# A fused linear-attention and MLP kernel: the transposes of x for units 5 and 6 on SyncE's DMA queue in place of TensorE

## The chip, the cores and the metric

The kernel runs on 1 core of a Trainium2 chip. The metric is the device time of one execution in microseconds (us). The kernel before took 170.78 us, the median of 3 runs (170.48 to 170.87).

## The reference

Two stages are fused. The first is a gated linear attention over 4 batches, 8 heads, 768 steps and a head size of 48; the second is a two-layer MLP with squared ReLU on its 3072 x 384 output.

```python
for t in range(S):                                   # S = 768
    state = alpha[:, :, t, :, None] * state + einsum('bhd,bhe->bhde', k[:, :, t], v[:, :, t])
    y[:, :, t] = einsum('bhd,bhde->bhe', q[:, :, t], state)
x = y.transpose(0, 2, 1, 3).reshape(B * S, H * D)    # 3072 x 384
h = x @ w_in                                         # 384 x 2048
r = maximum(h, 0); g = r * r
out = g @ w_out                                      # 2048 x 384
```

## The kernel before

The 3072 tokens are cut into 12 units of 256 tokens, numbered 0 to 11; four batches take turns, so unit g is chunk g // 4 of batch g % 4. For each unit g the kernel does, in this order (the names are those of the tables in `ORDERS`, and the lines those of the profile):

- `lda`, `ldk`, `ldq`, `ldv`: load alpha, k, q and v, 384 KB each, into one of four `raw` buffers, number g % 4 (L540).
- `pr`, `ln`, `m1`, `ei`, `ea`, `es`, `bk`, ...: the decays; `eqm0`, `eqm1` (L732) and `ekm` (L737) multiply them into q and k and write `qks`, buffer g % 3.
- `tr0`, `tr1` (L748): from unit 3 on, two DMA transposes on SyncE's queue turn `qks` into `kqt`, buffer g % 3.
- `p0` (L926): the scores on TensorE, which read `kqt`; `mk0`, `mk1` (L937) mask them.
- `y` (L818, L829, L797): the attention's output and the next state on TensorE; `xe` (L957) copies it as bf16 into `xbf`, buffer g % 2.
- `xt`: x, 128 x 768 in bf16, is turned for the MLP. Up to unit 6 TensorE does it with six 128 x 128 transposing matmuls (L972) into PSUM, and `xv` (L984) copies the result into the `xt` buffer g % 4. From unit 7 on a single DMA transpose on SyncE's queue (L978) writes that buffer directly, and there is no `xv`. The tuple `DMA_X` holds the units that take this second way.
- `s1_g_0` to `s1_g_7` (L1030): the first layer, six matmuls each, reading `xt`; `re` (L1038, L1040) is its ReLU and `sq` (L1052, L1048, L1051) the square.
- `s2_g_...` (L1168, L1096): the second layer, for units 3 to 10 by Strassen's scheme, whose sums are `ga`, `gb`, `gc` and whose results are gathered by `ca` to `cg`; `out` stores 384 KB.

The order of the work on every engine is written out by hand in five tables in `ORDERS`, one for each engine; each engine runs its row from left to right and waits on semaphores where it needs another's result. `fill` names small matmuls on zeros in the first 16 us (L1231). Several units are under way at a time: while TensorE computes the first layer of unit 5, the attention of unit 6 and the loads of units 7 and 8 are running. SyncE's table is one queue: whatever waits at its head holds everything behind it.

The switch between the two ways for x is in `output`:

```python
if g in DMA_X:
    to = XT[s][:].rearrange("p k j t -> p (k j t)").rearrange("p (a t) -> p a t", t=128)
    add("sp", lambda e: e.dma_start_transpose(to, src), 1300, p0 + 6700, reads=[("xbf", x2)],
        writes=[("xt", s)], name=f"xt{g}", dma=f"x{s}", lag=1400)
    return
add("pe", xtr, pe_ns(6, 128), p0 + 6700, reads=[("xbf", x2), ("ident",)], writes=[("ps", "X", 0)], name=f"xt{g}")
```

Of the kernel before, what the change touches and what calls it, by code (L numbers as in the profile page):

```python
# [34 lines left out]
        cd6 eqm0_10 eqm1_10 ga7_0 ce6 sa10 ga7_1 cg6 re8_4 cf6 re8_5 ca7 cb7 lb11 ekm11 eqm0_11 eqm1_11 mk0_10 cd7
        mk1_10 ce7 cf7 re9_1 ga8_1 cg7 re9_2 sa11 ca8 re9_4 mk0_11 re9_7 cb8 mk1_11 re10_0 cd8 ga9_1 ce8 gb9_1 re10_2
        ga9_0 cg8 cf8 re10_7 cb9 cc9 ga10_0 cd9 gc9_0 ce9 ga10_1 cf9 cg9 cb10 re11_4 gc10_0 cd10 ce10 cg10 re11_6
        sq11_7 cf10 oe11_0 oe11_11
    """,
    "pe": """  # L40
        fill512_0 fill512_1 fill512_2 fill512_3 fill512_4 fill512_5 fill256_6 m10_0 m11_0 fill512_7 tr00_0 tr10_0
        fill512_8 fill256_9 fill256_10 tr01_0 p0_0 tr11_0 kv0 fill256_11 p1_0 fill512_12 m11 y0 fill512_13 fill512_14
# [1 line left out]
        kv1 s1_0_3 y1 s1_0_4 s1_0_5 xt1 s1_0_7 s1_0_6 m1i2 s1_1_2 s1_1_1 m1s2 s1_1_0 s1_1_4 s1_1_5 s1_1_3 s1_1_7 tr0_2
        s1_1_6 s2_0_0_0 tr1_2 s2_0_0_1 s2_0_1_0 p0_2 s2_0_1_1 s2_0_0_2 s2_0_0_3 kv2 s2_0_1_2 m1i3 s2_0_1_3 s2_1_0_0
        s2_1_0_1 m1s3 y2 m1i4 s2_1_0_2 xt2 s2_1_0_3 s1_2_0 s1_2_1 s2_1_1_0 s2_1_1_1 s1_2_2 s1_2_3 p0_3 s2_1_1_2 s1_2_5
        s1_2_4 s2_1_1_3 y3 s1_2_6 s1_2_7 xt3 m1i5 s2_2_0_0 s1_3_1 s2_2_0_1 s1_3_0 p0_4 s2_2_0_2 s1_3_3 s2_2_0_3 s1_3_2
        s1_3_5 y4 s2_2_1_0 s1_3_4 m1i6 s1_3_7 xt4 s2_2_1_1 s2_2_1_2 s1_3_6 s2_2_1_3 s1_4_1 p0_5 s1_4_0 s2_3_m10 s1_4_3
        s2_3_m11 s1_4_2 y5 s2_3_m20 s1_4_4 m1i7 s2_3_m60 s2_3_m61 s2_3_m21 xt5 s1_4_6 s2_3_m70 s1_4_5 s2_3_m50
        s2_3_m71 s2_3_m51 s1_4_7 p0_6 s2_3_m40 s1_5_0 s1_5_1 s2_3_m30 s1_5_2 s2_3_m41 s1_5_3 s2_3_m31 y6 s2_4_m10  # L50
        s2_4_m60 s2_4_m11 s1_5_5 m1i8 xt6 s2_4_m61 s1_5_4 s2_4_m20 s2_4_m21 s1_5_7 s1_5_6 p0_7 s2_4_m70 s1_6_1 s1_6_0
        s2_4_m50 s2_4_m71 s2_4_m51 s1_6_2 y7 s2_4_m30 s2_4_m40 s2_4_m41 s1_6_3 m1i9 s1_6_4 s2_4_m31 s2_5_m60 s1_6_5
        s2_5_m10 s2_5_m11 s1_6_6 s1_6_7 s2_5_m61 p0_8 s2_5_m20 s2_5_m21 s1_7_1 s1_7_0 s2_5_m70 s2_5_m71 s1_7_3 s1_7_2
        s2_5_m50 s2_5_m51 s2_5_m40 y8 s2_5_m41 s2_5_m30 s1_7_4 s2_6_m60 m1i10 s2_5_m31 s1_7_5 s2_6_m61 s2_6_m10
        s2_6_m11 s1_7_6 s1_7_7 p0_9 s2_6_m20 s2_6_m70 s1_8_0 s2_6_m21 s2_6_m71 s1_8_1 s1_8_2 s2_6_m50 y9 s2_6_m51
        s2_6_m40 s1_8_3 s2_6_m30 s2_6_m31 s1_8_4 s2_6_m41 s2_7_m10 m1i11 s1_8_5 s2_7_m60 s2_7_m11 s2_7_m61 s1_8_6
        s2_7_m20 s1_8_7 s2_7_m70 s2_7_m21 p0_10 s2_7_m50 s2_7_m51 s2_7_m71 s1_9_0 s1_9_1 s2_7_m40 s2_7_m41 s1_9_2 y10
        s2_7_m30 s2_7_m31 s1_9_3 s2_8_m10 s2_8_m60 s2_8_m11 s1_9_5 s1_9_4 p0_11 s2_8_m20 s1_9_7 s2_8_m61 s2_8_m21
# [1205 lines left out]
```

## Time and profile before

| | |
|---|---|
| median of 3 runs | 170.78 us |
| the profiled execution | 169.46 us, of which 167.7 us from the first to the last instruction |
| granted TensorE clock | 1.000 |
| busy | TensorE 96%, VectorE 79%, ScalarE 72%, GpSimd 58% of the span |
| DMA moved | 32.80 MB, mean 196 GB/s |

In the profile's rows PE is TensorE, PEld its weight loads, DVE VectorE, ACT ScalarE, POOL GpSimd, and SPq the issues of DMAs on SyncE. A row of the timeline has the start, the duration, the engine, the source line, the operation and what it writes and reads; a trailing x2 joins two alike. An SPq row's duration is that of the issue alone; when the data have landed is told in the DMA view, as microseconds from the issue. Times are counted from the start of the span.

### The profile page before, as it was taken

The numbers are of one execution on the slowest core, as the hardware profiler recorded it, in microseconds if no ns is written. First come the engines' busy times: TensorE is split into PE (matmuls) and PEld (weight loads), VectorE is DVE, ScalarE is ACT, GpSimd is POOL, SyncE is SP. The second block draws the span as 40 slices with busy tenths as digits, with TensorE's granted clock in tenths as the row PEclk, the third lists the DMA queues.
The fourth block names the chain that finished last, engine by engine and source line by source line (L and its number), as shares of the span: only waits on it lengthen the run. The fifth ranks groups of instructions, "written<-read, shape, count | busy, mean of one in ns | idle before, by whom it ended". The sixth has DMA issues, their size and how long they took to land.

```text
span 167.7 us, 5626 instructions
## 1 busy us (share of the span) xinstructions
PE 160.9 (96%) x2431; PEld 139.6 (83%) x2431; DVE 131.9 (79%) x234; ACT 121.3 (72%) x214; POOL 96.8 (58%) x93
## 2 busy tenths in 40 slices
PE   7699999997999999999999999999999999999994
...
DMA  5999999999999999999999989989988500522022
GB/s 135 327 319 209 275 303 216 200 338 267 161 230 166 229 295 124 294 160 263 282 163 327 241 136 336 141 193 334 133 203 139 148 10 4 152 87 94 0 98 94
DMA packets 68232, 32.80 MB, mean 196 GB/s; under 512 B 64144, under 2 KB 65168, under 8 KB 68208
## 3 DMA queue, kind: packets, MB, share of 16 engines
...
q14 instruction: 5, 0.04, 0.1%
HBM read 25.17 MB, written 4.72 MB: 178 GB/s over the span
## 4 chain that ended last, share of the span: by engine, by line
PE 75%; DMA 15%; POOL 4%; DVE 3%; issue 1%; ACT 1%
PE psWH L1030 32%; PE psO L1096 13%; PE psWH L1096 10%; PE psO L1168 7%; DMA win<-in_moe_w_in_dram 7%; DMA wout<-in_moe_w_out_dram 5%; DMA raw<-in_alpha_dram 3%; PE psX L829 2%; PE psX L926 2%; PE psZ L797 2%; POOL raw L540 2%; PE psX L818 2%; PE psX L998 2%; PE psZ L926 1%; PE psX L972 1%; POOL win L508 1%
## 5 line engine op out<-in xcount | busy, mean ns | idle before, releaser
L1030 PE MATMUL psWH<-xt,win 128*128 128x256 bf16 x552 | 71.7, 273 | 0.2 <-DMA win<-in_moe_w_in_dram 0.2
L1030 PEld LDWEIGHTS psWH<-xt,win 128*128 128x128 bf16 x552 | 60.1, 129 | 2.1 <-DVE xt L984 0.4
L1038 ACT ACTIVATE rr<-psWH 128x512 bf16<-128x512 f32 x70 | 40.9, 595 | 18.3 <-PE psWH L1030 17.2
L1052 ACT ACTIVATE gt<-rr 128x1024 bf16<-128x1024 bf16 (+1 forms) x38 | 35.1, 940 | 2.8 <-PE psWH L1096 1.6
L1051 POOL TENSOR_TENSOR gt<-rr 128x512 bf16<-128x512 bf16 (+1 forms) x13 | 18.6, 1432 | 14.8 <-ACT rr L1038 9.7
L1082 POOL TENSOR_TENSOR gt<-sg,gt 128x512 bf16<-128x512 bf16 x10 | 12.0, 1202 | 12.6 <-DVE sg L1080 12.6
L1040 DVE TENSOR_SCALAR rr<-psWH 128x512 bf16<-128x512 f32 x22 | 15.0, 685 | 5.1 <-PE psWH L1030 5.0
L1168 PE MATMUL psO<-wout,gt 128*128 128x384 bf16 x96 | 18.4, 326 | 0.0
L937 DVE TENSOR_TENSOR pm<-psZ,caus 128x1024 bf16<-128x1024 f32 x12 | 14.6, 1218 | 1.9 <-PE psZ L926 1.9
L937 DVE TENSOR_TENSOR pm<-psX,caus 128x1024 bf16<-128x1024 f32 x12 | 14.6, 1215 | 0.6 <-PE psZ L926 0.5
L1096 PE MATMUL psWH<-sw,gt 128*128 128x192 bf16 x128 | 14.8, 246 | 0.0
L1096 PE MATMUL psO<-wout,gt 128*128 128x192 bf16 x128 | 14.7, 246 | 0.0
L1083 POOL TENSOR_TENSOR sh<-gt 128x512 bf16<-128x512 bf16 x11 | 14.2, 1298 | 0.7 <-DVE gt L1082 0.5
L1168 PEld LDWEIGHTS psO<-wout,gt 128*128 128x128 bf16 x96 | 8.8, 98 | 4.6
L686 POOL TENSOR_TENSOR ek<-ek,raw 128x384 f32<-128x384 f32 x7 | 7.1, 1008 | 9.6 <-ACT ek L679 9.6
L1127 DVE TENSOR_TENSOR osb<-psWH,osb 128x192 f32<-128x192 f32 x24 | 8.4, 350 | 5.0 <-PE psWH L1096 4.9
L737 DVE TENSOR_TENSOR qks<-raw,ek 128x768 bf16<-128x768 f32 x11 | 11.7, 1063 | 0.4 <-ACT ek L644 0.4
L1080 DVE TENSOR_TENSOR sg<-gt 128x1024 bf16<-128x1024 bf16 x14 | 10.6, 754 | 0.9 <-PE psO L1096 0.9
L1096 PEld LDWEIGHTS psWH<-sw,gt 128*128 128x128 bf16 x128 | 10.9, 98 | 0.3
L1096 PEld LDWEIGHTS psO<-wout,gt 128*128 128x128 bf16 x128 | 10.6, 98 | 0.5
L957 ACT ACTIVATE xbf<-psX 128x768 bf16<-128x768 f32 x11 | 8.9, 806 | 2.9 <-PE psX L818 1.7
L732 DVE TENSOR_TENSOR qks<-raw,eq 128x384 bf16<-128x384 f32 x18 | 10.4, 604 | 0.7 <-DMA raw<-in_q_dram 0.7
...
## 6 DMA issues: line engine op xcount, KB each, us to landing
out_dram<-osb SPq DMA_DIRECT2D x11, 384.0 KB, 4.8
raw<-in_alpha_dram SPq DMA_DIRECT2D x10, 384.0 KB, 5.1
raw<-in_q_dram SPq DMA_DIRECT2D x10, 384.0 KB, 5.5
raw<-in_v_dram SPq DMA_DIRECT2D x10, 384.0 KB, 4.8
raw<-in_k_dram SPq DMA_DIRECT2D x9, 384.0 KB, 5.2
...
raw<-in_k_dram POOLq DMA_DIRECT2D x3, 384.0 KB, 6.4
raw<-in_alpha_dram POOLq DMA_DIRECT2D x2, 384.0 KB, 6.0
```

The costliest lines, as they stand in the source:

```text
L737: add("dve", lambda e, a=a, E=E: e.tensor_tensor(QKS[qs][:, a, :, :, 0:D], RAW[r][:, 1 + a].rearrange("p h j d -> p j h d"), E[la][:].rear ...
L937: add("dve", lambda e, hf=hf, psT=psT: e.tensor_tensor(PM[pm][:, hf].rearrange("p r n j t -> p (r n) (j t)"), psT[:, :, :].rearrange("p r ...
L1030: ins = pe.matmul(psF[:, i * T:(i + 1) * T], WIN[:, kk, hidden(fj)], mov, start=(kk == 0), stop=(kk == KT - 1))
L1038: add("act", lambda e, psF=psF, rr=rr: e.activation(rr, psF, AF.Relu), act_ns(512), pu + 600, reads=[keyF], writes=[("rr", rb, half)], nam ...
L1040: alts={"dve": (lambda e, psF=psF, rr=rr: e.tensor_scalar(rr, psF, 0.0, None, ALU.max), dve_ns(512))})
L1051: alts={"pool": (lambda e, dst=dst, sq=sq: e.tensor_tensor(dst, sq, sq, ALU.mult), 200 + k * 840), "act": (lambda e, dst=dst, sq=sq: e.act ...
L1052: "act": (lambda e, dst=dst, sq=sq: e.activation(dst, sq, AF.Square), act_ns(k * 512))})
L1080: ga = lambda e, us=us: e.tensor_tensor(SG[:, us], view(us, 128, [[0, 2], [1, 128]]), view(us, 0, [[384, 2], [1, 128]]), ALU.subtract)
L1082: gb = lambda e, us=us: e.tensor_tensor(G4[:, us, 0, 1], SG[:, us, 1], G4[:, us, 0, 0], ALU.subtract)
L1083: gc = lambda e, us=us: e.tensor_tensor(SH[:, us], G4[:, us, 1, 0], G4[:, us, 0, 1], ALU.add)
L1096: ins = pe.matmul(psS, left(u), right(u), start=(first and u == 0), stop=(u == nu - 1), skip_group_check=True)
L1168: ins = pe.matmul(psS, GT[gt][:, fj, j, :], WOUT[:, fj, :], start=(fj == 0), stop=(fj == FT - 1))
```

## The change

`DMA_X` gets the units 5 and 6, so their two groups of six transposing matmuls leave TensorE, their two copies `xv5` and `xv6` leave VectorE, and two DMA transposes come onto SyncE's queue. The tables are changed with it, in one stretch that begins around the end of unit 3's first layer and ends at unit 6's (on SyncE between `out0_1` and `xt8`); behind it they are as before. Four `fill` matmuls are added in the first 16 us and some change their size. In the same stretch other operations move by a few places in their tables, and two change engine: `ca3` goes from ScalarE to VectorE and `gb5_1` from VectorE to GpSimd.

```diff
-    DMA_X = (7, 8, 9, 10, 11)
+    DMA_X = (5, 6, 7, 8, 9, 10, 11)
...
     "sp": """
-        ldk6 ldq6 tr1_5 tr0_5 ldv6 lda7 ldk7 lda8 tr0_6 tr1_6 ldv7 ldq7 ldq8 out1_1 ldk8 tr0_7 tr1_7 ldv8 lda9 ldk9
+        ldk7 ldk6 lda7 ldq6 tr1_5 tr0_5 ldv6 lda8 ldv7 ldq7 tr0_6 tr1_6 ldq8 xt5 ldk8 ldk9 lda9 out1_1 tr0_7 tr1_7
+        ldv8 xt6 lda10 ldq9 ldv9 tr0_8 tr1_8 out2_1 xt7 out3_1 lda11 tr1_9 tr0_9 ldk10 xt8 ldv10 ldq10 ldk11 ldq11
```

SyncE's queue behind the store of unit 0 is the first place. raw2 is the buffer of unit 6, raw3 of unit 7, raw0 of unit 8; kqt2 and kqt0 belong to units 5 and 6, xt1 to unit 5. Before, from `ldk6` to `ldq8`:

```order
L540 DMA raw2<-in_k_dram 128x8x96
L540 DMA raw2<-in_q_dram 128x8x96
L748 DMA_TRANSPOSE kqt2<-qks2 128x16x64 x2
L540 DMA raw2<-in_v_dram 128x8x96
L540 DMA raw3<-in_alpha_dram 128x8x96
L540 DMA raw3<-in_k_dram 128x8x96
L540 DMA raw0<-in_alpha_dram 128x8x96
L748 DMA_TRANSPOSE kqt0<-qks0 128x16x64 x2
L540 DMA raw3<-in_v_dram 128x8x96
L540 DMA raw3<-in_q_dram 128x8x96
L540 DMA raw0<-in_q_dram 128x8x96
```

The same place now, from `ldk7` to `xt5`:

```order
L540 DMA raw3<-in_k_dram 128x8x96
L540 DMA raw2<-in_k_dram 128x8x96
L540 DMA raw3<-in_alpha_dram 128x8x96
L540 DMA raw2<-in_q_dram 128x8x96
L748 DMA_TRANSPOSE kqt2<-qks2 128x16x64 x2
L540 DMA raw2<-in_v_dram 128x8x96
L540 DMA raw0<-in_alpha_dram 128x8x96
L540 DMA raw3<-in_v_dram 128x8x96
L540 DMA raw3<-in_q_dram 128x8x96
L748 DMA_TRANSPOSE kqt0<-qks0 128x16x64 x2
L540 DMA raw0<-in_q_dram 128x8x96
L978 DMA_TRANSPOSE xt1<-xbf1 128x6x128
```

Two loads of unit 7 (k and alpha) have moved ahead of the transposes of unit 5, two more (v and q) ahead of those of unit 6, and `xt5` stands behind exactly the eleven rows that were there before, in another order.

The second place is SyncE's queue behind that. raw1 is the buffer of unit 9, kqt1 of unit 7, xt2 of unit 6. Before, from `out1_1` to `ldk9`:

```order
L1184 DMA out_0_dram<-osb1 128x768
L540 DMA raw0<-in_k_dram 128x8x96
L748 DMA_TRANSPOSE kqt1<-qks1 128x16x64 x2
L540 DMA raw0<-in_v_dram 128x8x96
L540 DMA raw1<-in_alpha_dram 128x8x96
L540 DMA raw1<-in_k_dram 128x8x96
```

Now, from `ldk8` to `xt6`:

```order
L540 DMA raw0<-in_k_dram 128x8x96
L540 DMA raw1<-in_k_dram 128x8x96
L540 DMA raw1<-in_alpha_dram 128x8x96
L1184 DMA out_0_dram<-osb1 128x768
L748 DMA_TRANSPOSE kqt1<-qks1 128x16x64 x2
L540 DMA raw0<-in_v_dram 128x8x96
L978 DMA_TRANSPOSE xt2<-xbf0 128x6x128
```

Again the same six rows stand ahead of the new one, `xt6`.

The third place is TensorE around the first use of x of unit 5; xt0 and xt1 are the x of units 4 and 5, kqt0 is read by the scores `p0_6`. Before:

```order
L1030 MATMUL psWH<-xt0,win 128x256 x6
L926 MATMUL psX<-kqt0 64x128 x16
L926 MATMUL psZ<-kqt0 64x128 x16
L1096 MATMUL psWH<-sw,gt1 128x192 x4
L1030 MATMUL psWH<-xt1,win 128x256 x12
```

Now:

```order
L926 MATMUL psX<-kqt0 64x128 x16
L926 MATMUL psZ<-kqt0 64x128 x16
L1030 MATMUL psWH<-xt0,win 128x256 x6
L1096 MATMUL psO<-wout,sh 128x192 x4
L1030 MATMUL psWH<-xt1,win 128x256 x12
```

One group of the first layer of unit 4 has moved behind the scores of unit 6. Between the output of unit 5 and the first row with xt1 stand as many groups of each layer as before (four of six matmuls on L1030, nine of four on L1096), and the transposes of L972 are gone.

More of the change, by code (lines that the diff above doesn't have):

```diff
@@ L17 @@
         re2_5 lm5 lm6 xe3 ln5 re2_7 ei5 ea5 ec5 sq2_5 re3_1 re3_0 re3_3 es5 oe2_0 re3_2 ln6 sq3_3 xe4 ei6 ea6 ec6
-        re3_7 sq3_5 es6 sq3_7 re3_6 oe2_1 re4_1 re4_0 sq4_1 lm7 ca3 re4_2 ln7 xe5 ei7 re4_3 ea7 sq4_3 ec7 re4_5 re4_6
-        lm8 re4_7 es7 sq4_7 re5_0 re5_1 sq4_5 re5_2 sq4_6 re5_3 ln8 xe6 ei8 re5_5 ea8 re5_4 es8 re5_7 cc4 re5_6 sq5_3
-        re6_0 lm9 sq5_5 ln9 re6_1 re6_2 lm10 re6_3 ei9 re6_4 ea9 re6_5 sq6_1 re6_6 re6_7 sq6_3 es9 re7_1 re7_0 cc5
+        sq3_5 es6 re3_7 re3_6 sq3_7 oe2_1 re4_1 re4_0 lm7 sq4_1 re4_2 ln7 xe5 ei7 re4_3 sq4_3 ea7 ec7 re4_5 sq4_5
+        re4_6 es7 re4_7 lm8 re5_0 re5_1 ln8 sq4_7 sq4_6 re5_3 re5_2 xe6 lm9 ei8 ea8 re5_5 re5_4 es8 re5_7 re5_6 sq5_3
+        cc4 re6_0 sq5_5 re6_1 ln9 re6_2 lm10 re6_3 ei9 re6_4 ea9 re6_5 sq6_1 re6_6 re6_7 sq6_3 es9 re7_1 re7_0 cc5
         sq6_5 re7_3 re7_2 ln10 xe8 sq7_1 ei10 ea10 re7_4 re7_5 ca6 lm11 re7_6 re7_7 es10 re8_0 cc6 re8_1 sq7_7 sq7_5
@@ L35 @@
[L35 to L38, printed above, removed]
+        eqm0_5 sq3_1 sa5 re3_5 sc5 re3_4 xv4 lb6 eqm1_6 eqm0_6 gb3_0 ekm6 mk0_5 mk1_5 pr7 ga3_1 sa6 ca3 ws3_1 re4_4
@@ new lines @@
+        sc6 cc3 cb3 ekm7 lb7 cd3 ce3 mk1_6 eqm0_7 eqm1_7 ga4_0 mk0_6 cf3 cg3 gb4_0 ga4_1 sa7 gb4_1 sc7 ca4 lb8 ekm8
+        cb4 eqm0_8 mk0_7 eqm1_8 mk1_7 cd4 ce4 ga5_0 sa8 xe7 sq5_6 ga5_1 cf4 cg4 lb9 ekm9 ca5 gc5_1 eqm1_9 cb5 mk0_8
+        eqm0_9 mk1_8 cd5 gc5_0 ga6_0 ce5 sa9 cf5 ga6_1 gb6_1 gc6_0 cg5 sq7_3 lb10 cb6 ekm10 sq7_6 mk0_9 mk1_9 cd6
+        eqm0_10 eqm1_10 ga7_0 ce6 sa10 ga7_1 cg6 re8_4 cf6 re8_5 ca7 cb7 lb11 ekm11 eqm0_11 eqm1_11 mk0_10 cd7 mk1_10
+        ce7 cf7 re9_1 ga8_1 cg7 re9_2 sa11 ca8 re9_4 mk0_11 re9_7 cb8 mk1_11 re10_0 cd8 ga9_1 ce8 gb9_1 re10_2 ga9_0
@@ L44 @@
[L44 to L58, printed above, removed]
@@ L64 @@
-        s2_11_1_1
+        fill512_0 fill512_1 fill512_2 fill512_3 fill512_4 fill512_5 fill512_6 fill256_7 m10_0 m11_0 fill512_8
+        fill512_9 tr00_0 tr10_0 fill512_10 fill256_11 fill256_12 tr01_0 p0_0 tr11_0 kv0 fill256_13 p1_0 fill512_14
+        fill256_15 m11 fill256_16 y0 fill512_17 fill512_18 fill256_19 fill256_20 tr0_1 xt0 tr1_1 fill512_21 fill512_22
+        fill512_23 fill256_24 p0_1 s1_0_2 s1_0_0 s1_0_1 kv1 s1_0_3 y1 s1_0_4 s1_0_5 xt1 s1_0_7 s1_0_6 m1i2 s1_1_2
+        s1_1_1 m1s2 s1_1_0 s1_1_4 s1_1_5 s1_1_3 s1_1_7 tr0_2 s1_1_6 s2_0_0_0 tr1_2 s2_0_0_1 s2_0_1_0 p0_2 s2_0_1_1
@@ new lines @@
+        s2_0_0_2 s2_0_0_3 kv2 s2_0_1_2 m1i3 s2_0_1_3 s2_1_0_0 s2_1_0_1 m1s3 y2 m1i4 s2_1_0_2 xt2 s2_1_0_3 s1_2_0
+        s1_2_1 s2_1_1_0 s2_1_1_1 s1_2_2 s1_2_3 p0_3 s2_1_1_2 s1_2_5 s1_2_4 s2_1_1_3 y3 s1_2_6 s1_2_7 xt3 m1i5 s2_2_0_0
+        s1_3_1 s2_2_0_1 s1_3_0 p0_4 s2_2_0_2 s1_3_3 s2_2_0_3 s1_3_2 s1_3_5 y4 s2_2_1_0 s1_3_4 m1i6 s2_2_1_1 xt4
+        s2_2_1_2 s1_3_7 s1_3_6 s2_2_1_3 s1_4_1 p0_5 s1_4_0 s2_3_m10 s1_4_3 s2_3_m11 s1_4_2 y5 s1_4_4 m1i7 s2_3_m60
+        s2_3_m61 s2_3_m20 s2_3_m21 s1_4_6 s1_4_5 s2_3_m50 s2_3_m70 s2_3_m51 s2_3_m71 p0_6 s1_4_7 s2_3_m30 s1_5_0
@@ new lines @@
+        s1_5_1 s2_3_m31 s2_3_m40 s1_5_2 s2_3_m41 s1_5_3 y6 s2_4_m10 s2_4_m60 s2_4_m11 m1i8 s1_5_5 s1_5_4 s2_4_m61
+        s2_4_m20 s2_4_m21 s1_5_7 s1_5_6 p0_7 s2_4_m70 s1_6_1 s1_6_0 s2_4_m71 s2_4_m50 s2_4_m51 s1_6_2 y7 s2_4_m40
+        s1_6_3 s2_4_m41 m1i9 s2_4_m30 s1_6_4 s2_4_m31 s1_6_5 s2_5_m60 s2_5_m10 s1_6_6 s2_5_m11 s1_6_7 s2_5_m61 p0_8
+        s2_5_m20 s2_5_m21 s1_7_1 s1_7_0 s2_5_m70 s2_5_m71 s1_7_3 s1_7_2 s2_5_m50 s2_5_m51 s2_5_m40 y8 s2_5_m41
+        s2_5_m30 s1_7_4 s2_6_m60 m1i10 s2_5_m31 s1_7_5 s2_6_m61 s2_6_m10 s2_6_m11 s1_7_6 s1_7_7 p0_9 s2_6_m20 s2_6_m70
@@ new lines @@
+        s1_8_0 s2_6_m21 s2_6_m71 s1_8_1 s1_8_2 s2_6_m50 y9 s2_6_m51 s2_6_m40 s1_8_3 s2_6_m30 s2_6_m31 s1_8_4 s2_6_m41
+        s2_7_m10 m1i11 s1_8_5 s2_7_m60 s2_7_m11 s2_7_m61 s1_8_6 s2_7_m20 s1_8_7 s2_7_m70 s2_7_m21 p0_10 s2_7_m50
+        s2_7_m51 s2_7_m71 s1_9_0 s1_9_1 s2_7_m40 s2_7_m41 s1_9_2 y10 s2_7_m30 s2_7_m31 s1_9_3 s2_8_m10 s2_8_m60
+        s2_8_m11 s1_9_5 s1_9_4 p0_11 s2_8_m20 s1_9_7 s2_8_m61 s2_8_m21 s1_9_6 s2_8_m50 s1_10_1 s1_10_0 s2_8_m70
+        s2_8_m51 s2_8_m71 s1_10_2 s1_10_3 s2_8_m40 s2_8_m41 y11 s2_8_m30 s2_8_m31 s1_10_5 s2_9_m10 s2_9_m11 s1_10_4
@@ L65 @@
+        s1_10_7 s2_9_m20 s2_9_m60 s2_9_m21 s2_9_m61 s1_10_6 s2_9_m70 s2_9_m50 s2_9_m51 s1_11_0 s1_11_1 s2_9_m71
+        s1_11_2 s1_11_3 s2_9_m40 s2_9_m41 s2_9_m30 s2_9_m31 s1_11_4 s2_10_m10 s2_10_m11 s2_10_m60 s1_11_5 s2_10_m61
+        s2_10_m20 s2_10_m21 s2_10_m70 s2_10_m71 s2_10_m50 s1_11_6 s2_10_m51 s1_11_7 s2_10_m30 s2_10_m31 s2_10_m40
+        s2_10_m41 s2_11_0_0 s2_11_0_1 s2_11_0_2 s2_11_0_3 s2_11_1_0 s2_11_1_1
     """,
```

25 lines of the change are left out of this document (7 added, 18 removed).

## The prediction

> **What bounds the kernel now.** The page comes first, for the engine that never rests.
>
> ```profile
> span 167.7 us, 5626 instructions
> PE 160.9 (96%) x2431; PEld 139.6 (83%) x2431; DVE 131.9 (79%) x234; ACT 121.3 (72%) x214; POOL 96.8 (58%) x93
> ...
> PE   7699999997999999999999999999999999999994
> ...
> DMA  5999999999999999999999989989988500522022
> ```
>
> TensorE is busy in all slices from 42 us (the eleventh, at 4.2 us a slice) to the last. The DMA engines are busy too, up to slice 31, which is 130 us. So two resources run full side by side, and a change that moves work from the one to the other has to be looked at on both. The view by stretches of time tells how full (columns: length, then busy time of PE, PEld, DVE, ACT and POOL, TensorE's clock, DMA share, GB/s):
>
> ```profile
> 57.00:62.00 5.00, 5.00 (x102) 4.07 (x95) 4.52 (x7) 3.64 (x8) 2.65 (x3) 1.00 1.13 335
> 62.00:63.00 1.00, 1.00 (x12) 0.90 (x11) 1.00 (x3) 0.52 (x1) 0.88 (x1) 1.00 0.63 138
> 66.00:67.00 1.00, 1.00 (x10) 0.74 (x9) 1.00 (x2) 1.00 (x3) 0.00 (x0) 1.00 0.59 94
> 77.00:82.00 5.00, 5.00 (x78) 4.72 (x76) 4.72 (x8) 4.64 (x9) 4.08 (x4) 1.00 1.13 334
> 87.00:92.00 5.00, 5.00 (x79) 4.73 (x77) 4.41 (x6) 4.09 (x8) 3.27 (x5) 1.00 1.16 317
> 97.00:98.00 1.00, 1.00 (x14) 0.99 (x11) 1.00 (x3) 0.73 (x3) 1.00 (x2) 1.00 1.03 144
> ```
>
> Where loads flow, 317 to 335 GB/s go through, with the share over 1: a load of 384 KB (0.393 MB) takes 1.2 us and there is no room beside it. In the stretch that the change touches I see two short dips, at 62 and at 66 us, where the queue changes between loads and transposes.
>
> Then SyncE's queue and TensorE's scores and first layers, from the timeline. The rows of SyncE are issues:
>
> ```profile
> 57.83 1.07 SPq L540 DMA_DIRECT2D raw<-in_q_dram  x1
> 61.40 3.17 SPq L748 DMA_TRANSPOSE kqt<-qks  x2
> 62.69 1.88 SPq L748 DMA_TRANSPOSE kqt<-qks  x1
> 75.94 1.67 SPq L540 DMA_DIRECT2D raw<-in_q_dram  x1
> 77.66 1.15 SPq L1184 DMA_DIRECT2D out_dram<-osb  x1
> 86.62 1.33 SPq L540 DMA_DIRECT2D raw<-in_k_dram  x1
> 94.62 1.59 SPq L748 DMA_TRANSPOSE kqt<-qks  x1
> 96.26 2.04 SPq L978 DMA_TRANSPOSE xt<-xbf  x1
> ...
> 67.50 0.42 PE L926 MATMUL psX<-kqt 64*64 64x128 bf16 x16
> 78.75 0.93 PE L1030 MATMUL psWH<-xt,win 128*128 128x256 bf16 x7
> 89.62 1.47 PE L1030 MATMUL psWH<-xt,win 128*128 128x256 bf16 x12
> ```
>
> They are `ldq6`, `tr1_5` and `tr0_5` as one row, `tr0_5` alone, `ldq8`, `out1_1`, `ldk9`, `tr1_8` and `xt7`; on TensorE `p0_5`, `s1_5_0` and `s1_6_1`, the first reader of x of unit 6. The DMA view, asked for windows that hold one issue alone, has the time from issue to landing (last column); for `ldq6`, `tr0_5`, `ldq8`, `ldk9`, `tr1_8` and `xt7`:
>
> ```profile
> raw<-in_q_dram SPq DMA_DIRECT2D x1, 384.0 KB, 6.3
> ...
> kqt<-qks SPq DMA_TRANSPOSE x1, 4.4
> ...
> raw<-in_q_dram SPq DMA_DIRECT2D x1, 384.0 KB, 6.4
> ...
> raw<-in_k_dram SPq DMA_DIRECT2D x1, 384.0 KB, 4.9
> ...
> kqt<-qks SPq DMA_TRANSPOSE x1, 4.3
> ...
> xt<-xbf SPq DMA_TRANSPOSE x1, 3.6
> ```
>
> So `ldq6` lands at 64.1, `tr0_5` at 67.1, `ldq8` at 82.3, `ldk9` at 91.5, `tr1_8` at 98.9 and `xt7` at 99.9. `p0_5` starts at 67.50, 0.4 us after the landing it needs: the queue has almost no lead over TensorE.
>
> **What leaves TensorE and VectorE.**
>
> ```profile
> L972 PE MATMUL psX<-ident,xbf 128*128 128x128 bf16 x42 | 3.5, 220 | 0.0
> ...
> 73.78 0.49 PE L1096 MATMUL psO<-wout,gt 128*128 128x192 bf16 x4
> 74.11 0.50 PE L972 MATMUL psX<-ident,xbf 128*128 128x128 bf16 x6
> 74.45 0.28 PE L1030 MATMUL psWH<-xt,win 128*128 128x256 bf16 x1
> ...
> 64.95 0.55 DVE L984 COPY xt<-psX 128x768 bf16<-128x768 bf16 x1
> ...
> 15.01 0.92 PE L1231 MATMUL psO<-zero 128*128 128x512 bf16 x4
> ```
>
> The first row groups all seven units' transposes, 7 x 6 matmuls; the others are single places of the timeline. Matmuls overlap, so a group's price is from its start to the next start: 74.45 - 74.11 = 0.34 us. Two groups are 0.68 us, all of it on the engine that is never idle; this is the whole possible gain. The two copies of 0.55 us leave VectorE, which is not the bound: nothing by themselves. The front is set by loads, not by the fills:
>
> ```profile
> 8.79 11.97 DMA win<-in_moe_w_in_dram
> ...
> 21.04 8.26 DMA wout<-in_moe_w_out_dram
> ...
> 29.32 5.54 DMA raw<-in_alpha_dram
> ```
>
> That is the chain of waits from 8.8 to 34.9 us; four fills more lie beside it and I price them at nothing; four in a row took 0.92 us at 15 us, which would be the cost if each met work that was ready. `ca3` on VectorE and `gb5_1` on GpSimd lie on engines with room (4.72 and 4.08 of 5.00 us at 77 to 82): nothing, and 0.3 us either way as a bound, half a copy as above.
>
> **What it costs on the queue.** A transfer of x took 99.9 - 98.9 = 1.0 us behind another transpose. I count the rows ahead of each reader, since the queue works them off one after the other and is full.
>
> First, the scores `p0_5`. Ahead of `tr0_5` there are now two loads more: 2 x 1.2 = 2.4 us. What can be absorbed is the dip at 62 us, (335 - 138) / 335 of a us = 0.6 us. So `tr0_5` lands 1.8 to 2.4 us later, at 68.9 to 69.5, and TensorE, which is there at 67.50, waits 1.4 to 2.0 us; everything else on it is queued behind. `ldq6` comes later by as much, at 65.9 to 66.5, and holds `eqm` of unit 6 and the masks behind it on VectorE. The masks wait for the scores anyway, as they did before,
>
> ```profile
> 68.19 1.22 DVE L937 TENSOR_TENSOR pm<-psZ,caus 128x1024 bf16<-128x1024 f32 x1 [0.56 <-PE psZ L926]
> ```
>
> so this has no charge of its own.
>
> Second, `s1_5_0`. `xt5` stands behind the same eleven rows as `ldq8` did, plus itself: it lands at 82.3 + 1.0 = 83.3 at the latest of this reckoning. From that go the dip, 0.6, and up to 1.2 for the store of unit 1 that shared the engines with `ldq8` and now comes later: 81.5 to 83.3. TensorE started `s1_5_0` at 78.75. The landing pushes it 2.7 to 4.6 us, and with the second group saved behind it the end moves by +2.4 to +4.2. The wait at `p0_5` lies inside this one and isn't added.
>
> Third, `s1_6_1`. `xt6` stands behind the six rows that ended with `ldk9`, and behind `xt5`: 91.5 + 2 x 1.0 = 93.5, less the dip 92.9. It was started at 89.62 before, so the end moves by +3.3 to +3.9. Two things bound this further. `xt5` now lies between two loads, and such a change costs: at 66 us, behind the transposes of unit 5, (335 - 94) / 335 = 0.7 us were lost. That gives up to +4.6. On the low side, the second place's +2.4.
>
> The trace moved 144 GB/s in a stretch of transposes alone (97 to 98 us), less than half of the loads' 317 to 335. The Trainium skill (Advanced Engine Details and Errata, section X-Bar Transpose (TRN2)) says the opposite of such a row: a transposing DMA is about as fast as an ordinary one. By that rule a transfer of x, half a load's bytes, would be an estimated 0.6 us, and the third place would give +2.5 to +3.1; the trace does not agree, and I take its 1.0 us.
>
> Later places do not bind: `xt7` has one load (`ldv9`, 1.2) and two transposes of x (2.0) more ahead of it, 99.9 + 3.2 = 103.1, and its reader, which is behind `s1_6_1` on TensorE, is itself pushed by some 3.3 us:
>
> ```profile
> 101.31 1.31 PE psWH L1030 x12
> ```
>
> This row of the chain is that reader's, 101.3 + 3.3 = 104.6, past the landing. Nor is anything won back: behind the stretch the order is the same and TensorE has no idle time to give.
>
> The sum is the latest of the three places: +3.3 us, between +2.4 and +4.6. The profiled execution took 169.46 us, 1.3 us less than the median of 170.78, so a profile after would show about 172.8 and the median **174.1 us**.
>
> **The rivals.** A measurement of this kernel can tell about 0.2%, 0.34 us, from no change.
>
> (a) *As forecast*, waits at the places above: 173.2 to 175.4, chance 0.60.
>
> (b) *The x transposes hide, the early loads do not.* If packets of a transpose slip in beside loads, only the wait at `p0_5` is left: 1.4 to 2.0 less 0.68, +0.7 to +1.3, 171.5 to 172.1; partly hidden, up to 173.2. For it: the share goes over 1. Against: it does so with loads alone as well, at 87 to 92 us. Chance 0.20.
>
> (c) *Each change between loads and transposes costs its 0.7 us*, both at `xt5` and at `xt6`: above 175.4. Chance 0.05, since the dip at 66 us isn't seen behind every transpose.
>
> (d) *Faster.* The queue runs its loads ahead in the 2.5 us between 58.9 (`ldq6` issued) and 61.4, when SyncE issues nothing, and the whole 0.68 us is won: 170.1. It decides at `tr0_5`: landing by 67.5, the scores do not wait. For it: SyncE is idle there. Against: the DMA engines are not; the windows at 57 to 62 us show 335 GB/s, what had been issued was still being moved. Chance 0.11.
>
> (e) Both about cancel, 170.4 to 171.1: chance 0.04.
>
> **Numbers.** (a) is the likeliest and gives 174.1. The range 171.2 to 175.4 holds (a) and (b) and leaves out (c), (d) and (e), 0.20. Faster 0.11, same 0.04, slower 0.85.
>
> **What would show it.** In the profile after: TensorE, busy in every slice from 42 us on before, has idle time at L926 (scores of unit 5, near 69 us, released by a DMA of `kqt`) and at L1030 near 82 and 93 us (released by a DMA of `xt`), together 3.5 to 4.5 us; its busy time is 0.7 us less; L972 has 30 instructions instead of 42. I am wrong if `tr0_5` lands before 68 us, if the waits at L1030 are absent, or if they are there and the time is given back behind 100 us.

## The result, and the profile after

The changed kernel takes 174.80 us (median of 4, 174.36 to 175.25), the kernel before 170.63 us (median of 4, 169.30 to 170.87): a ratio of 1.0261, interval 1.0211 to 1.0310. It is 4.2 us slower; the interval makes that 3.6 to 5.3 us. The profiled execution after took 174.97 us, the one before 169.46 us. Here and below a time is the median of all executions, while a ratio and its interval leave out those more than 1.5% above the fastest of the same kernel, so the two can differ a little.

The page after, in the rows that answer to those of before:

```profile
span 173.3 us, 5608 instructions
PE 161.8 (93%) x2421; PEld 139.6 (81%) x2423; DVE 133.2 (77%) x232; ACT 121.6 (70%) x213; POOL 97.7 (56%) x94
...
PE   7999999997999995995997999999999999999992
...
DMA  5999999999898999999999995899979520522022
```

The row of TensorE has three holes behind the eleventh slice, where before there was none; they lie at 65 to 69, 78 to 82 and 91 to 95 us. The view of TensorE's waits from 42 us on had no row at all before. Now it has three (total in us, how many, the longest):

```profile
PE psWH L1030 <- DMA xt<-xbf: 2.7, 2, 1.5
PE psX L926 <- DMA kqt<-qks: 2.0, 1, 2.0
PE psX L926 <- DVE osb L1127: 0.5, 1, 0.5
```

The timeline of TensorE has the places, each with its wait in brackets (`p0_5`, `p0_6`, `s1_5_0`, `s1_6_1`; the second, for a gathered result, was not forecast):

```profile
69.28 0.42 PE L926 MATMUL psX<-kqt 64*64 64x128 bf16 x16 [2.00 <-DMA kqt<-qks]
...
79.25 0.42 PE L926 MATMUL psX<-kqt 64*64 64x128 bf16 x16 [0.49 <-DVE osb L1127]
...
82.56 1.48 PE L1030 MATMUL psWH<-xt,win 128*128 128x256 bf16 x12 [1.53 <-DMA xt<-xbf]
...
94.47 1.25 PE L1030 MATMUL psWH<-xt,win 128*128 128x256 bf16 x10 [1.21 <-DMA xt<-xbf]
```

The chain of waits gives issue and time to landing of the three transfers they waited for, `tr0_5`, `xt5` and `xt6`:

```profile
65.29 3.95 DMA kqt<-qks
...
78.01 4.42 DMA xt<-xbf
...
90.25 4.08 DMA xt<-xbf
```

They landed at 69.24, 82.43 and 94.33. The four waits add up to 5.2 us. Behind them nothing comes back: the scores of unit 9 start 4.85 us later than before (116.60 against 111.75), and so do every later unit's, within 0.01 us.

Profiled executions differ by up to 1.7 us at the scores of unit 4 (`p0_4`, 55.7 to 57.4 us), ahead of all that the change moves but the fills. So in the traces below I count what a kernel loses **behind p0_4**: its distance to before at `p0_9` less that at `p0_4`. After loses 5.0 us there (from -0.17 to +4.85): nearly all of the 5.2 us of waits, so little of the 0.68 us that was to be saved on TensorE shows. The timed comparisons contain this scatter in their intervals; theirs for after, 3.6 to 5.3 us, holds the 5.0 as well as the 4.2.

### The profile page after: what moved, and what is told of

The parts are those of the page before. It is cut to its first block, busy times and chain, and to the rows that moved or that the text cites. A ratio compares the mean times of both kernels' runs of the same rounds, so it can differ in the third digit from the quotient of the medians.

```text
span 173.3 us, 5608 instructions
## 1 busy us (share of the span) xinstructions
PE 161.8 (93%) x2421; PEld 139.6 (81%) x2423; DVE 133.2 (77%) x232; ACT 121.6 (70%) x213; POOL 97.7 (56%) x94
## 4 chain that ended last, share of the span: by engine, by line
PE 81%; DMA 9%; ACT 4%; DVE 3%; issue 1%; SPq 0%; ACTq 0%
PE psWH L1030 32%; PE psO L1096 11%; PE psWH L1096 8%; PE psO L1168 8%; DMA xt<-xbf 5%; PE psZ L797 2%; DMA kqt<-qks 2%; PE psX L926 2%; PE psX L829 2%; DMA raw<-in_alpha_dram 2%; PE psX L818 2%; PE psX L998 2%; PE psZ L926 1%; PE psO L1231 1%; PE psWH L1168 1%; PE psZ L760 1%
## 5 line engine op out<-in xcount | busy, mean ns | idle before, releaser
L1030 PE MATMUL psWH<-xt,win 128*128 128x256 bf16 x552 | 71.4, 273 | 2.9 <-DMA xt<-xbf 2.7
L1030 PEld LDWEIGHTS psWH<-xt,win 128*128 128x128 bf16 x552 | 60.1, 129 | 5.3 <-issue 1.9
L1082 POOL TENSOR_TENSOR gt<-sg,gt 128x512 bf16<-128x512 bf16 x11 | 13.1, 1197 | 12.9 <-DVE sg L1080 12.9
L1096 PE MATMUL psWH<-sw,gt 128*128 128x192 bf16 x128 | 15.0, 246 | 0.0
L1096 PE MATMUL psO<-wout,gt 128*128 128x192 bf16 x128 | 14.7, 246 | 0.0
L1127 DVE TENSOR_TENSOR osb<-psWH,osb 128x192 f32<-128x192 f32 x24 | 8.4, 352 | 7.4 <-PE psWH L1096 7.2
L1083 POOL TENSOR_TENSOR sh<-gt 128x512 bf16<-128x512 bf16 x11 | 13.3, 1220 | 0.5 <-DVE gt L1082 0.4
L737 DVE TENSOR_TENSOR qks<-raw,ek 128x768 bf16<-128x768 f32 x11 | 12.3, 1115 | 0.7 <-ACT ek L644 0.4
L732 DVE TENSOR_TENSOR qks<-raw,eq 128x384 bf16<-128x384 f32 x18 | 11.0, 645 | 1.7 <-DMA raw<-in_q_dram 1.7
L1096 PEld LDWEIGHTS psWH<-sw,gt 128*128 128x128 bf16 x128 | 11.0, 98 | 0.2
L727 POOL CAST vbf<-raw 128x768 bf16<-128x768 f32 x9 | 8.2, 908 | 5.3 <-DMA raw<-in_v_dram 5.3
L1096 PEld LDWEIGHTS psO<-wout,gt 128*128 128x128 bf16 x128 | 10.7, 98 | 0.5
```

The lines of the kernel that those rows point to most:

```text
L732: add("dve", lambda e, j=j, dst=dst: e.tensor_tensor(dst, RAW[r][:, 2, :, j, :].rearrange("p (n x) d -> p n x d", x=2), EQ[la][:, j].rearr ...
L737: add("dve", lambda e, a=a, E=E: e.tensor_tensor(QKS[qs][:, a, :, :, 0:D], RAW[r][:, 1 + a].rearrange("p h j d -> p j h d"), E[la][:].rear ...
L1030: ins = pe.matmul(psF[:, i * T:(i + 1) * T], WIN[:, kk, hidden(fj)], mov, start=(kk == 0), stop=(kk == KT - 1))
L1082: gb = lambda e, us=us: e.tensor_tensor(G4[:, us, 0, 1], SG[:, us, 1], G4[:, us, 0, 0], ALU.subtract)
L1083: gc = lambda e, us=us: e.tensor_tensor(SH[:, us], G4[:, us, 1, 0], G4[:, us, 0, 1], ALU.add)
L1096: ins = pe.matmul(psS, left(u), right(u), start=(first and u == 0), stop=(u == nu - 1), skip_group_check=True)
```

## The experiments

Theory A is throughout the prediction's: what counts is each reader's place in SyncE's queue. Each experiment names its rivals itself; theory B, in e2 and e5 to e8, is that a transpose of x on SyncE's queue costs by itself, wherever it stands. Ratios are to the kernel before, timed beside it. The tables of `ORDERS` are shown cut to the names that move.

**e1, the loads alone.** Before, with SyncE's table of after, less `xt5` and `xt6`; x stays on TensorE.

```diff
-ldk6 ldq6 tr1_5 tr0_5 ldv6 lda7 ldk7 lda8 tr0_6 tr1_6 ldv7 ldq7 ldq8 out1_1 ldk8 tr0_7 ...
+ldk7 ldk6 lda7 ldq6 tr1_5 tr0_5 ldv6 lda8 ldv7 ldq7 tr0_6 tr1_6 ldq8 ldk8 ldk9 lda9 out1_1 tr0_7 ...
```

> The kernel before with one thing of the change alone: SyncE's queue has the changed order of loads and stores, but without the two transposes of x, which stay on TensorE; all other tables are those of before. Theory A (the queue is worked off one after the other, so what is put ahead of a reader's transfer delays the reader): the transposes of unit 5 land near 69.2 us instead of 67.1, the scores of unit 5 wait 1.5 to 2.1 us for them, the later readers are then covered by this delay, and the end moves by +1.4 to +2.1 us against before. Theory B (the transposes of x on the queue are the whole cost, the order of the loads is free): within 0.4 us of before. Theory C (the other tables or the fills cost it): as before too.

171.83 us, ratio 1.0094 (1.0059 to 1.0130). The waits of TensorE from 42 us on:

```profile
PE psX L926 <- DMA kqt<-qks: 1.1, 1, 1.1
PE psX L926 <- DVE qks L732: 0.2, 1, 0.2
```

`p0_5` starts at 69.09 (67.50 before); 0.5 of these 1.6 us this trace already had at `p0_4`, which is why its wait is 1.1 us and not A's 1.5 to 2.1. So the first place is real by itself: two loads ahead of a transpose that TensorE reads 0.4 us after it lands. The trace loses 1.1 us behind `p0_4`, the timing 1.6 us by the ratio (1.0 to 2.2), of the 4.2; the rest is left to x and the other edits.

**e3, x one place ahead.** After, with `xt5` ahead of `ldq8` and `xt6` ahead of `ldv8`.

```diff
-tr0_6 tr1_6 ldq8 xt5 ldk8 ... tr0_7 tr1_7 ldv8 xt6
+tr0_6 tr1_6 xt5 ldq8 ldk8 ... tr0_7 tr1_7 xt6 ldv8
```

> The changed kernel with the two transposes of x one place ahead: xt5 before ldq8, xt6 before ldv8, nothing else. Theory A: the scores of unit 5 still wait 2.0 us; xt5 lands near 80.2 instead of 82.4 and xt6 near 91.5 to 92.2 instead of 94.3, so the waits of the first layer fall from 1.5 and 1.2 us to under 0.4 each; the end moves by -2.0 to -2.7 us against the changed kernel, that is +1.4 to +2.2 against before. Theory B: it saves under 0.7 us, since the same two transposes stay on the queue. Theory C: no change, +4.2 against before.

173.00 us, ratio 1.0151 (1.0111 to 1.0190). One wait is left,

```profile
PE psX L926 <- DMA kqt<-qks: 2.4, 1, 2.4
```

and both at L1030 are gone: they hung on one load each. That is as A says; the time is not: by the ratio it is 2.6 us over before, 0.4 us above A's upper end. The windows of the profiled execution show something that A does not have. Row by row: after at 69 to 73 us, then e3 (after the five engines the column of TensorE's granted clock):

```profile
69.00:70.00 1.00, 0.72 (x34) 0.63 (x35) 1.00 (x2) 0.00 (x0) 0.02 (x1) 1.00 0.82 171
70.00:73.00 3.00, 3.00 (x58) 2.78 (x57) 3.00 (x5) 2.25 (x4) 0.82 (x1) 1.00 1.15 320
```

```profile
69.00:70.00 1.00, 0.95 (x35) 0.84 (x36) 0.85 (x2) 0.00 (x0) 0.00 (x0) 0.95 0.99 247
70.00:73.00 3.00, 3.00 (x18) 2.34 (x16) 3.00 (x4) 1.96 (x3) 0.82 (x1) 0.50 1.17 324
```

In e3 TensorE stood 2.38 us, and 0.8 us after it went on its clock was halved for 3.4 us: 18 matmuls in place of 58 in the 3 us shown. `y5` then started 3.21 us later than before where `p0_5` had started 1.55 later. After stood 2.00 us at the same place and kept its clock. This is a reason for this execution alone: two others of e3 with a mean clock of 1.000 took 171.92 and 173.29 us, so what lies above A's range in the timing isn't shown to be the clock.

**e4, light loads.** After, with six of the loads that stand ahead of the three readers' transfers (k7, alpha7, q8, k8, k9, alpha9, the names in `LIGHT`) cut to one head of eight; the other heads keep the values that stood in the buffer.

```diff
-            name = f"{nm}{g}"
+            name = f"{nm}{g}"; src, dst = (src[:, 0:1], dst[:, 0:1]) if name in LIGHT else (src, dst)
```

> The changed kernel with its queue relieved and its order kept: six loads (k and alpha of unit 7, q and k of unit 8, k and alpha of unit 9) move one head of eight, the other seven heads keep older values of the buffer; all instructions and waits are there. Theory A: what delayed the readers was bytes ahead of them; the scores of unit 5 wait under 0.3 us, the first layers of units 5 and 6 under 0.8 us together, and the end is at -0.7 to +0.3 us against before. Theory B': a transpose of x has a fixed latency or SyncE's issue holds it, whatever the load on the queue: the waits of 1.5 and 1.2 us at the first layers stay, and the end is at +2 us or more. Theory C: the end is at +4 us as without the relief.

170.14 us, ratio 1.0010 (0.9979 to 1.0041). The waits:

```profile
PE psX L926 <- DVE qks L732: 0.7, 1, 0.7
PE psWH L1030 <- DMA xt<-xbf: 0.3, 1, 0.3
```

The first lies at 48 us, ahead of all that moved, the second at 114. With after's order and after's x, the loss is gone once the bytes ahead are. So the loss is queueing on a queue full of loads; neither the edits on VectorE and GpSimd nor the fills cost anything that this shows. It does not tell the order of the loads from the transposes of x among them: the relief serves both.

**e2, x moved, loads kept.** Before's tables without the transposes of x on TensorE and their copies; `xt5` stands behind `tr1_6`, `xt6` behind `tr1_7`.

```diff
-tr0_6 tr1_6 ldv7 ldq7 ... tr0_7 tr1_7 ldv8
+tr0_6 tr1_6 xt5 ldv7 ldq7 ... tr0_7 tr1_7 xt6 ldv8
```

> The kernel before with the other thing alone: x of units 5 and 6 by SyncE's queue, all loads and stores in the order of before, each transpose of x directly behind the transposes of q and k of the next unit (xt5 behind tr1_6, xt6 behind tr1_7); the other tables are those of before without the two transposes and the two copies. Theory A: xt5 lands near 77.6 us, ahead of its reader at 78.4; xt6 near 89.9 to 90.6, its reader waits 0.5 to 1.2 us or the scores of unit 7 do; two transfers of 1.0 us against a lead of about 1 us and a saving of 0.68: the end moves by -0.5 to +0.9 us against before. Theory B: by +2 to +4 us. Theory C: by -0.7 us.

174.49 us, ratio 1.0242 (1.0195 to 1.0289), 4.1 us over before: A missed by far, and theory B's 2 to 4 us are nearly met. The loads stand where they stood, so x alone can cost as much as the whole change: e1's 1.6 us and e2's 4.1 are not two parts that add up to it. No wait at L1030 or L926 from a DMA; this one instead, and the timeline shows who made it, `eqm1_7` and `eqm0_7`, then the mask `mk0_6`, then `y6`:

```profile
PE psX L818 <- DVE pm L937: 2.4, 1, 2.4
```

```profile
81.12 2.74 DVE L732 TENSOR_TENSOR qks<-raw,eq 128x384 bf16<-128x384 f32 x2 [1.20 <-DMA raw<-in_q_dram]
83.78 1.21 DVE L937 TENSOR_TENSOR pm<-psX,caus 128x1024 bf16<-128x1024 f32 x1
...
85.05 0.19 PE L818 MATMUL psX<-sbd,kqt 64*128 64x48 bf16 x1 [2.38 <-DVE pm L937]
```

q of unit 7 landed 1.1 us later, behind `xt5`. VectorE's table has its two products ahead of a mask whose scores were there already. And again the clock was at 0.50 for 3.4 us behind a wait of 2.38 us. A looked at the readers of the transposes, not at those of the loads behind them.

**e5, e6, e7: that chain undone.** e5 is e2 with `mk0_6` ahead of `eqm1_7` on VectorE, e6 is e2 with `ldq7` ahead of `ldv7` on SyncE, e7 has both.

```diff
-dve: mk1_6 eqm1_7 eqm0_7 mk0_6
+dve: mk1_6 mk0_6 eqm1_7 eqm0_7
-sp: xt5 ldv7 ldq7
+sp: xt5 ldq7 ldv7
```

> Loads in the order of before, x of units 5 and 6 on SP right behind their unit's pair of transposes, and in VectorE's order the mask mk0_6 moved ahead of the two products of q of unit 7. Theory A (what is behind the queue's order decides; e2's excess was the mask held 2.7 us behind q7, which landed 1.1 us late): y6's wait for pm falls from 2.4 to under 0.4 us, xt5 and xt6 land near 77.3 and 91.0 as in e2, the clock stays 1.0 behind it; what may stay is the accumulation of units behind the products of q7, under 1 us. End 0.7 us less to 1.0 us more than before. Theory B (x on SP costs by itself, wherever it stands, as traffic beside the loads): 2 to 4 us more than before, as in e2.

> As e2, and on SP the load of q of unit 7 ahead of the load of v of unit 7. Theory A: q7 lands at 79.0 to 80.0 instead of 81.1, y6's wait for pm goes, the end 0.7 us less to 0.6 us more than before. Theory B: 2 to 4 us more than before.

> e5's and e6's edits together. Theory A: no wait over 0.4 us on TensorE behind 42 us, the end 0.7 us less to 0.4 us more than before (the 0.68 us of the 12 transposes is the most it can gain). Theory B: 2 to 4 us more.

e5 173.88 us, 1.0229 (1.0174 to 1.0283); e6 172.89 us, 1.0165 (1.0102 to 1.0227); e7 173.13 us, 1.0173 (1.0118 to 1.0228). The wait for the mask went in all three, and A's times, at most 1.0 us over before, are missed again: by the ratios they are 3.9, 2.8 and 3.0 us over, all within theory B's 2 to 4. e6 has one larger wait left behind `p0_4`, which e5 and e7 have too, at 1.4 us, beside one of 1.0 and 1.2 us for a gathered result (`osb`, L1127):

```profile
PE psWH L1030 <- ACT rr L1038: 1.0, 1, 1.0
```

**e8, unit 6 alone.** Before, with only `xt6` on SyncE, behind `tr1_7`.

> Before with only unit 6's x on SP, right behind its unit's pair of transposes; loads and all else in the order of before, 6 transposes of 128x128 fewer on TensorE. Theory A: nothing ahead of 86 us moves, q7 lands at 80.0 as in before, xt6 lands near 90 (its reader stood at 89.6 in before, so a wait of 0 to 0.6 us), the end 0.3 us less to 0.6 us more than before. Theory B: 1 to 2 us more.

171.31 us, ratio 1.0073 (1.0028 to 1.0119), which is 1.2 us over before, B's 1 to 2 and not A's 0.6 at most; behind `p0_4` it loses 0.8 us, with the same wait (0.9). So one transpose of x, `xt6` alone, brings this wait. The timeline follows it back: on GpSimd the copy of v of unit 8 waits for its load and holds the product of the decay (L658) that ScalarE needs ahead of that ReLU. Before, then e8:

```profile
84.66 1.26 SPq L540 DMA_DIRECT2D raw<-in_v_dram  x1
...
89.82 0.82 POOL L727 CAST vbf<-raw 128x768 bf16<-128x768 f32 x1
91.71 1.38 POOL L658 TENSOR_TENSOR prd<-raw 128x384 f32<-128x384 f32 x1
```

```profile
85.15 2.02 SPq L978 DMA_TRANSPOSE xt<-xbf  x1
87.22 0.58 SPq L540 DMA_DIRECT2D raw<-in_v_dram  x1
...
91.32 0.82 POOL L727 CAST vbf<-raw 128x768 bf16<-128x768 f32 x1 [1.03 <-DMA raw<-in_v_dram]
93.59 1.44 POOL L658 TENSOR_TENSOR prd<-raw 128x384 f32<-128x384 f32 x1
```

With one transpose of x ahead, the load is issued 2.56 us later than before (0.45 of it e8's lag at the transposes ahead) and the product of the decay is 1.9 us late. The transfer itself took 0.8 us; SyncE was 2.02 us at issuing it.

**e9, e10: GpSimd's order.** `gc4_1` ahead of `vc8`, in e8 and in e6.

```diff
-sq5_7 vc8 gc4_1 pr9
+sq5_7 gc4_1 vc8 pr9
```

> e8 (only unit 6's x on SP) with one step of GpSimd's order exchanged: the product gc4_1 (sh, line 1083) ahead of the copy vc8 of v of unit 8 (line 727), which in e8 waited 1.03 us for v and held the prefix product of the decay (prd, line 658) and, through it, ScalarE and TensorE (0.9 us at 96). Theory A (e8's loss is the load behind xt6, handed on by the fixed orders): prd starts at 92.5 to 92.9 instead of 93.6, TensorE's wait for rr at 96 falls from 0.86 to under 0.3 us, and the end comes 0.4 to 0.9 us ahead of e8's, 0.3 us less to 0.6 us more than before. Theory B (the transfers of the x transposes slow TensorE's operands or others directly): as e8.

> e6 (x of both units on SP behind their pairs, q7 ahead of v7) with the same exchange on GpSimd. Theory A: TensorE's wait for rr at 96.7 falls from 1.05 to under 0.4 us, the end 0.6 to 1.1 us ahead of e6's, between 0.5 us less and 1.0 us more than before. Theory B: as e6, 2 to 3 us more than before.

e9 171.85 us, 1.0104 (1.0063 to 1.0146); e10 172.68 us, 1.0159 (1.0112 to 1.0206). The wait for `rr` is gone in both, as A said, but the time is not told apart from e8's and e6's, where A had it better by 0.4 to 1.1 us: in e9 TensorE now waits 0.8 us at 101.9 us for a gathered result (`osb`), in e10 1.2 us at 84 us for the copy of v of unit 7, whose load e6's exchange had put back. The waits change place, the lost time of the queue stays. I found no order that wins with x of unit 5 or 6 on SyncE.

**e11, a light transpose.** e8, with `xt6` cut to the first 128 of 768 columns; the rest of `xt` keeps what stood there.

> e8 with the SP transpose of unit 6's x cut to the first 128 of its 768 columns (the other five blocks of xt keep what stood there). From the end of unit 7's second transpose to the end of v8's data e8 took 3.03 us, before 1.25 us: 0.83 us of it the transfer, 0.25 us a gap, and v8's own 1.97 us in place of 1.29 us. If the queue pays for bytes (theory A1), it comes down to 1.4 to 1.7 us; if it pays for a transpose and the load behind it as such (theory A2), to 2.1 to 2.5 us, and v8 still lands 0.8 us or more later than in before; TensorE's wait for rr then falls from 0.86 us to 0.0 to 0.3 us.

171.06 us, ratio 1.0051 (1.0020 to 1.0082), not told apart from e8's. From the end of `tr1_7`'s data to the end of v8's it took 2.85 us, by the packets' times: above both theories' ranges, and A1 falls. Five sixths of the bytes taken away won 0.18 us of the 1.78 us that e8 has over before. SyncE's rows:

```profile
84.84 1.93 SPq L978 DMA_TRANSPOSE xt<-xbf  x1
86.81 0.58 SPq L540 DMA_DIRECT2D raw<-in_v_dram  x1
```

The issue takes as long as with all columns. The windows, before, e8 and e11 (last column GB/s):

```profile
87.00:88.00 1.00, 1.00 (x13) 1.00 (x11) 1.00 (x2) 0.93 (x2) 0.10 (x1) 1.00 1.16 303
88.00:89.00 1.00, 1.00 (x28) 0.84 (x29) 0.81 (x2) 0.88 (x4) 0.17 (x1) 1.00 1.17 323
89.00:90.00 1.00, 1.00 (x36) 0.91 (x25) 0.60 (x1) 1.00 (x2) 1.00 (x2) 1.00 1.16 321
```

```profile
87.00:88.00 1.00, 1.00 (x13) 0.99 (x12) 0.50 (x2) 0.96 (x3) 0.68 (x1) 1.00 1.26 277
88.00:89.00 1.00, 1.00 (x11) 0.93 (x9) 1.00 (x3) 0.91 (x2) 0.00 (x0) 1.00 0.44 75
89.00:90.00 1.00, 1.00 (x38) 0.81 (x37) 0.60 (x2) 1.00 (x4) 0.78 (x1) 1.00 0.91 212
```

```profile
87.00:88.00 1.00, 1.00 (x13) 1.00 (x11) 0.82 (x2) 0.86 (x3) 0.36 (x1) 1.00 0.15 31
88.00:89.00 1.00, 1.00 (x24) 0.84 (x26) 1.00 (x2) 1.00 (x4) 0.10 (x1) 1.00 0.63 132
```

Against before, e8 lacks 26 + 248 + 109 = 383 GB/s over a us each, 1.2 us at 323 GB/s; e11 lacks 272 + 191 in two rows, 1.4 us. The hole in the DMA engines' work is there with a small transfer as with a large one. It fits that SyncE is busy issuing while what it had issued runs out. By the packets' times, in e2, e6, e8, e9, e10 and e11 the first data of v8 come 1.25 to 1.30 us after the start of its issue, as if nothing were ahead of it; before it was 2.5 us. Why an issue takes 2.0 us here and 1.3 us in after (78.01 and 90.25, loads ahead of it) is open. For TensorE these tenths mattered: in e11's trace the wait for `rr` is gone and nothing is lost up to `p0_9` (-0.2 us, where e8 loses 0.8). Behind it the trace has a wait of 1.0 us at y10 for v, which I do not explain.

**e12, the fills alone.** Before, with after's 25 fills in place of 21.

> Before with only TensorE's filling products of the first 16 us as the changed kernel has them (25 in place of 21: 8 in place of 7 ahead of the first product of the decay); nothing else is moved. The prediction set this edit at nothing, with 0.92 us as its bound. Theory A (nothing, as the prediction has it): within 0.3 us of before. Theory B (with 7 of them TensorE stands 0.6 to 0.8 us ahead of the first product of the decay and in most runs reaches full clock only about 9 us on; with 8 it stands 0.2 us and reaches it by 7 us): the first scores p0_0 start at 8.4 to 8.7 us, as in the changed kernel, where most profiles of before's order have 9.1 to 9.4; 0.3 to 0.8 us less than before. Theory C (the fills stand in the way): 0.2 to 0.9 us more than before.

169.79 us, ratio 0.9977 (0.9943 to 1.0011): -0.4 us, not told apart from nothing. `p0_0` starts at 8.55 us, which is where B put it (after 8.60; e1 9.36 and e8 9.30, with before's fills, though before's own profile has 8.44). That the fills gain up to half a us is possible, and not shown. C falls.

## Why the prediction was right

It named the direction, the three places and the cause, and the time came out 0.7 us above its 174.1, inside its range. That it came so near is in part luck. It was added up on the profiled execution of before, and that one lies 1.2 us under the median of its kernel (169.46, 170.63), while the one after lies at it: profile against profile the kernel is 5.5 us slower, where the sum had 3.3 and 4.6 as its bound. Two terms were too favourable, the saving and the transposes of x on the queue.

*What leaves TensorE, a term that was too large.* L972 has 30 instructions (42 before). Their price of 0.34 us a group was read from start to start, and taking a group away saves less. Before, then e8, where on TensorE nothing but unit 6's group is gone:

```profile
85.16 0.33 PE L668 MATMUL psZ<-lab,linc 128*128 128x384 bf16 x1
85.32 0.50 PE L972 MATMUL psX<-ident,xbf 128*128 128x128 bf16 x6
85.66 0.49 PE L1096 MATMUL psWH<-sw,gt 128*128 128x192 bf16 x4
```

```profile
85.74 0.33 PE L668 MATMUL psZ<-lab,linc 128*128 128x384 bf16 x1
86.04 0.50 PE L1096 MATMUL psWH<-sw,gt 128*128 128x192 bf16 x4
```

From L668 to L1096 it is 0.50 us before and 0.30 in e8: the matmul ahead now takes 0.30 us to the next start, not 0.16, and 0.2 us are won. Unit 5's group, the same way, wins 0.15 us (`p0_5` to `p0_6`: 10.33 us before, 10.18 in e7). Both are 0.35 us, half of the 0.68. In after even less is left: its four waits are 5.2 us and its loss 5.0. TensorE's busy time did not fall by 0.7 us either, as it was to do; the page has 161.8 us against 160.9. Up to 42 us it is 1.2 us more (38.90, 37.67), where e1 with before's fills has 38.91 too, so this isn't shown to be the change; from there on it is 0.3 us less (122.90, 123.24).

*What was priced at nothing.* e4 has all those edits (`xv`, `ca3`, `gb5_1`, fills), and stands at 1.0010 with 1.0 us of waits: together they cost nothing that can be told. The fills alone are e12.

*First place.* `tr0_5` at 68.9 to 69.5, wait 1.4 to 2.0: it landed at 69.24 and the wait was 2.00. That this wait is real without x is e1; rival (d), on the side of faster, decided at 67.5 and fell there.

*Second place.* `xt5` at 81.5 to 83.3: 82.43. `s1_5_0` started 3.8 us later than before, inside the 2.7 to 4.6; its own wait was 1.53, since the earlier ones had already put TensorE off.

*Third place, the term that was too small.* `xt6` at 92.9 to 93.5: 94.33, and the end moved by 4.85, past the 3.3 to 3.9 and the bound of 4.6. (Of 3.3 to 3.9 the sum took the lower end, and gave no reason.) Its sum was 91.5 for the six rows ahead, less 0.6 for the dip, and 1.0 each for `xt5` and `xt6`. e1 has the same rows without x. The issue of `ldv8`, the last of the six, and its time to landing in e1, then in after:

```profile
85.65 1.28 SPq L540 DMA_DIRECT2D raw<-in_v_dram  x1
...
raw<-in_v_dram SPq DMA_DIRECT2D x1, 384.0 KB, 4.6
```

```profile
88.80 1.41 SPq L540 DMA_DIRECT2D raw<-in_v_dram  x1
...
raw<-in_v_dram SPq DMA_DIRECT2D x1, 384.0 KB, 4.7
```

Without x they have landed at 90.3, 1.2 us ahead of 91.5: the dip is won, and as much again, so the prediction was 0.6 us too careful with the rows ahead. With the two transposes of x `xt6` lands 4.1 us behind that, where the sum had 1.0 for each. By the packets' times the data of the six rows end 3.4 us later than in e1 (93.12, 89.69). Of that, 0.6 us are there ahead of `xt5` already (end of `tr1_6`'s data: 78.68, 78.05). 1.9 us lie from there to the end of k8's, where `xt5` stands (4.36 us against 2.43). 0.8 us lie in `ldv8`, whose data took 2.09 us against 1.26; those of `xt6`, which stands behind it, began at 92.51, ahead of its end. In the same way q8's data, ahead of `xt5`, took 2.47 us against 1.26. So `xt5` cost 1.9 us and not 1.0, and `xt6`'s 0.9 us behind `ldv8` fits its 1.0 only if that load's 0.8 us are not its doing; this isn't shown. The prediction knew such a loss, from the change between loads and transposes at 66 us, and took it for a bound of 0.7 us, not for likely. Rival (c) charged it twice, and the time stayed just short of (c)'s 175.4.

*Rivals.* (b), x hidden and only `p0_5` late, gave 171.5 to 172.1; e1, which has only that wait, is there, and after lies 3 us above it. (a) holds. "Nothing is won back behind the stretch" holds to 0.01 us. What (a) stands on, that the place in the queue alone decides, does not hold beyond this order: e2, e5, e6 and e7 have no wait of TensorE for a transposing DMA left and still lose 2.8 to 4.1 us. A transpose of x also delays the loads behind it, and their readers hold others up, as e2 and e8 show; not every part of that loss is followed up.

*The rule weighed.* The Trainium skill (Advanced Engine Details and Errata, X-Bar Transpose (TRN2)) has transposes as fast as ordinary DMAs. In after, the 5 us from 87 on, with both of unit 7's transposes in them, moved 138 GB/s; before, which had almost only loads there, moved 317. The row after:

```profile
87.00:92.00 5.00, 5.00 (x71) 4.93 (x65) 4.61 (x10) 4.38 (x9) 3.48 (x3) 1.00 1.07 138
```

The trace does not agree, and here the rule's 0.6 us for a transfer of x would have made the sum worse: `xt5` cost the queue 1.9 us.
